# A hand-planned attention and two-layer kernel: weight preparation moved from GpSimd to VectorE, batch 0 turned with a diagonal factor, and a planner with other costs

## The chip, the core and the metric

The kernel runs on one core of one Trainium2 chip. A core has TensorE (PE), VectorE (DVE), ScalarE (ACT), GpSimd (POOL) and SyncE (SP), which issues the transfers here. Each engine takes its instructions in the order in which they were written. The metric is device time in microseconds (us) for one launch, lower is better: the median of the runs shown. A difference of about 0.5% is what a measurement of this kernel can tell from none.

## What is computed

```python
# q, k, v: (4, 12, 448, 64) fp32; w_in: (768, 2048); w_out: (2048, 768); alpha: (2048,)
scores = q @ k.T / 8
scores = cap * tanh(scores / cap)
attn   = exp(scores - max(scores)); attn = attn / (sum(attn) + 1e-9)
x      = (attn @ v) with the heads side by side        # (1792, 768)
h      = x @ w_in
g      = max(h, 0) + alpha * min(h, 0)
out    = g @ w_out                                     # (1792, 768)
```

The weights come as 64-bit floats, which the kernel reads as pairs of 32-bit integers.

## The kernel before

**Stages.** The four batches go through attention, then the first product (`mm1`), then the second (`mm2`). Attention works on pairs of heads, six pairs ("units") a batch. Batches 1 to 3 (`attention`) use fp16 pairs, a high and a low part of each number: q and k are scaled and split into `nat`, turned by a transfer into `qkTs`, multiplied on TensorE (L713), put through tanh (L501), row maximum (L506), exp (L513) and a factor per row (L518, L520). The weighted rows are split into `pw` (three buffers), turned by transfers into `ptall`, and multiplied with v (L585). Batch 0 (`attention32`) stays in fp32: q and k are turned on TensorE (L447, L448), the scores are fp32 products (L654), the rows of exp are scaled in place by their factor (in `steps`, `scaled`, L376 on VectorE), turned on TensorE against the identity (`turn_32`, L550), copied out of PSUM (L368) and multiplied with v (L599).

**Weights.** Each of the 16 chunks of `w_in` and of `w_out` is loaded as integers into `wp` and made into fp32 by `to_f32`: a shift and a mask (L826), the sign (L830), and the lowest bits. The lowest bits come in one of two ways: "fused", one VectorE instruction (L836), or a shift on VectorE (L839) and an add on GpSimd (L841). Then `split_w` makes an fp16 pair of each chunk, again in one of two ways: "direct" (the high part from the scaled chunk, L374 or L376, and the low part in one VectorE instruction with two inputs, L382), or scaled in place, copied (L368 or L370) and subtracted on GpSimd (L379). The constants XI, XO, AI and AO say which share of the chunks goes the fused or direct way: 0 and 0.25 for the bits of w_in and w_out, 0 and 0.75 for their splits. The scale of all w_out chunks (`s_wo`, L933) needs every chunk's norm, so `mm2` can't start before all of them are converted.

**What sets the order.** Every operation goes into a list by `Plan.op` with a priority, the engines that may do it, an assumed duration on each, and the regions that it reads and writes. `Plan.order` then plays the engines forward in time with these durations: a free engine takes the ready operation of the smallest number, an operation that ACT or POOL could do too is put back on DVE by PEN or PEN2, and the order found is the order in which the instructions are emitted. A wrong duration does no harm to the result, but the order is then made for another time table than the chip's. While the planned time is below FILL_END (87 us) and TensorE has nothing to do, the planner puts in "fills" (L980): small fp16 products of the identity with itself that nobody reads.

Of the kernel before, what the change touches and what calls it, by code (L numbers as in the profile page):

```python
# [29 lines left out]
PEN = 114.44  # L30
PEN2 = 133.12
B0_P = -3.48
LD_P = 2.02
LO_P = -51.36
MM_P = 203.41
X_P = 1.06
ST_P = 0.96
ST1_P = 5.53
PV_P = 22.36
QK_P = 10.39  # L40
V_P = 16.33
WI_P = 18.58
WI_S = 5.11
A_S = 7.06
MM1_P = 0.37
WO_P = 102.99
WO_S = 1.76
WT_P = 137.29
WT_S = 3.72
B1_P = 75.7  # L50
B_S = 31.76
EVAC_P = 57.51
# [5 lines left out]
XI = 0  # L58
XO = 0.25
AI = 0  # L60
AO = 0.75
# [3 lines left out]
FILL_END = 87045.86  # L65
# [10 lines left out]
class Plan:  # L76
# [15 lines left out]
    def op(self, prio, times, fn, r=(), w=(), rows=1.0):  # L92
        o = lambda: None
        o.prio, o.times, o.fn, o.rows, o.idx = prio, times, fn, rows, len(self.ops)
# [24 lines left out]
    def order(self):  # L119
# [6 lines left out]
        warm, win, busy = False, 0, 0.0  # L126

# [34 lines left out]
        while todo:  # L162
# [10 lines left out]
            for e in free:  # L173
# [3 lines left out]
                while ready[e]:  # L177
# [54 lines left out]
def kernel(  # L232
# [79 lines left out]
    mxt = ct([NF, 128], F32, "mxt")  # L312
    vs16 = ct([P, 2, 2, 2 * NCH * D], F16, "vs16")
# [28 lines left out]
    def allmax(prio, src, rows, r, first, w):  # L342
# [14 lines left out]
        op(prio, {"dve": 350}, reduce, r=[h], w=[tr])  # L357
        op(prio, {"pe": 100}, lambda e: nc.tensor.matmul(  # L358
            ps_p[h.slot][:, 256:256 + m], ones[:m], diag if m > 1 else top, start=True, stop=True), r=[tr], w=[h])
        op(prio, {"dve": 100}, lambda e: first(ps_p[h.slot][:, 256:256 + m]), r=[h], w=w)  # L360
# [60 lines left out]
    def vbatch(b):  # L421
# [8 lines left out]
        for pair in range(NPAIR):  # L430
# [3 lines left out]
            op(prio + 0.4 * pair, {"dve": 600}, lambda e, pair=pair, rv=rv: absmax(t[:CP, pair:pair + 1], rv),  # L434
               r=[m], w=[(u.tok, pair, pair + 1)])
# [41 lines left out]
    def steps(u, prio, n, S_, s_ns, sr_, scale, dma):  # L477
# [3 lines left out]
        for i0 in range(0, nb, 2):  # L481
# [15 lines left out]
            else:  # L497
# [3 lines left out]
            op(pr, {"act": 90 + 400 * m}, lambda e, s=s, t=t, m=m: nc.scalar.activation(  # L501
# [14 lines left out]
            op(pr, {"act": 735 * m}, exp, r=[mr], w=tr + [(("sums", u.idx % 3), c, c + 1) for c in blocks])  # L516
# [11 lines left out]
    blk_no = [0]  # L528
# [15 lines left out]
    def turn_32(u, pr, c, t, tr):  # L544
# [483 lines left out]
```

## Time and profile before

| what | value |
|---|---|
| median of 3 runs | 784.52 us (783.15 to 786.89) |
| the profiled execution | 784.08 us, its span from the first instruction to the last 782.3 us |
| busy in the span | PE 704.1, DVE 563.7, ACT 451.8, POOL 207.3 us |
| mean granted clock of TensorE | 0.954 of full speed |

The span is cut below at three marks: 261 us, when the scale of w_out is ready; 291 us, when the last chunk of w_out is split; 360 us, when the first product of batch 1 with w_in starts. Busy times are shares of the span and say nothing on which engine was waited for; the rows on the chain that ended last and on single waits do. A matmul's end is modelled in the trace, so for TensorE only stretches are summed.

### The profile page before, as it was taken

What the parts mean: (1) busy time and instruction counts of PE and PEld (TensorE: products, weight loads), DVE (VectorE), ACT (ScalarE), POOL (GpSimd) and SP (SyncE); (2) the same over time, 40 slices, a digit from 0 to 9 for tenths busy, and PEclk for the clock granted to TensorE, in tenths of its full rate; (3) what the DMA queues carried; (4) which work ended last, traced back from release to release, by engine and by line L of the source; (5) the groups of instructions that cost most, each with busy time, mean ns of one, the idle gap of its engine ahead of it and who ended that gap; (6) DMA issues with size and microseconds to landing.
All of it is one profiled execution on the core that took longest, in us unless ns stands there. A gap on an engine that the chain in (4) does not pass through costs nothing. (4 is left out here: it accounts for less than half of the span.)

```text
span 782.3 us, 12555 instructions
## 1 busy us (share of the span) xinstructions
PE 704.1 (90%) x4532; PEld 415.2 (53%) x4532; DVE 563.7 (72%) x1200; ACT 451.8 (58%) x877; POOL 207.3 (27%) x217
## 2 busy tenths in 40 slices
PE   8988967898988588959999999899999999999997
PEld 5646544476765245534444455455445555555664
DVE  4799997999998997887899877459879741443000
ACT  3767665798754874757686666457765821332010
POOL 1478463656653221100333300002222100000000
PEclk9999977899999689988999999999999999999999
DMA  9984523368775439997588887798658760000001
GB/s 212 241 256 126 169 75 100 107 149 175 176 172 126 91 75 175 205 177 160 113 135 158 157 171 148 144 173 143 107 110 146 130 116 20 21 1 1 21 21 40
DMA packets 227933, 98.61 MB, mean 126 GB/s; under 512 B 191456, under 2 KB 224160, under 8 KB 227872
## 3 DMA queue, kind: packets, MB, share of 16 engines
q1 hardware_dynamic: 227872, 97.82, 59.0%
q8 instruction: 35, 0.57, 0.3%
q14 instruction: 26, 0.21, 0.1%
HBM read 45.82 MB, written 5.51 MB: 66 GB/s over the span
## 5 line engine op out<-in xcount | busy, mean ns | idle before, releaser
L730 PE MATMUL p<-xring,wi 128*128 128x448 f16 (+2 forms) x1440 | 229.8, 319 | 3.6 <-POOL wi L379 2.5
L771 PE MATMUL p<-wp,gall 128*128 128x384 f16 x1344 | 227.9, 330 | 4.4 <-POOL wp L379 2.0
L730 PEld LDWEIGHTS <-wi 128*128 128x128 f16 x1440 | 138.0, 99 | 87.7 <-issue 4.7
L771 PEld LDWEIGHTS <-gall 128*128 128x128 f16 x1344 | 131.2, 99 | 95.7 <-issue 11.7
L513 ACT ACTIVATE tall<-tall,mxs,small 128x448 f32<-128x448 f32 x126 | 94.3, 750 | 22.2 <-POOL mxs L508 21.7
L382 DVE SCALAR_TENSOR_TENSOR pw<-tall,rr,pw 128x448 f16<-128x448 f32 x126 | 91.2, 737 | 12.5 <-ACT pw L374 12.1
L508 POOL TENSOR_SCALAR mxs<-mxs,small 128x2 f32<-128x2 f32 (+1 forms) x85 | 37.8, 444 | 229.0 <-DVE mxs L506 183.2
L379 POOL TENSOR_TENSOR gall<-gr,gall 128x192 f16<-128x192 f32 (+4 forms) x62 | 58.5, 947 | 115.5 <-ACT gall L368 73.8
L740 DVE SCALAR_TENSOR_TENSOR gr<-p,ca_g,gr 128x448 f32<-128x448 f32 (+2 forms) x80 | 46.5, 582 | 53.5 <-ACT gr L374 53.5
L374 ACT ACTIVATE pw<-tall,rr 128x448 f16<-128x448 f32 x95 | 61.8, 661 | 38.4 <-DMA ptall<-pw 25.4
L506 DVE TENSOR_REDUCE mxs<-tall 128x2 f32<-128x896 f32 x72 | 68.1, 957 | 17.5 <-ACT tall L501 17.5
L713 PE MATMUL s<-qkTs 128*128 128x448 f16 (+1 forms) x288 | 63.2, 384 | 19.3 <-DMA qkTs<-nat 18.5
L501 ACT ACTIVATE tall<-s,ams 128x896 f32<-128x896 f32 (+1 forms) x72 | 64.2, 904 | 24.5 <-PE s L713 22.8
L374 ACT ACTIVATE gr<-p,cs_g 128x448 f32<-128x448 f32 (+2 forms) x66 | 35.4, 537 | 46.8 <-PE p L730 44.9
L368 ACT ACTIVATE gall<-gr 128x384 f16<-128x384 f32 (+4 forms) x76 | 32.9, 438 | 40.4 <-DVE gr L740 40.4
L585 PE MATMUL p<-ptall,vs 112*64 112x448 f16 (+1 forms) x456 | 47.9, 352 | 2.2 <-DMA ptall<-pw 0.9
L374 ACT ACTIVATE wp<-p,small 128x384 f32<-128x384 f32 x20 | 11.5, 577 | 65.4 <-PE p L771 65.4
L713 PEld LDWEIGHTS <-qkTs 128*128 128x128 f16 (+1 forms) x288 | 22.8, 105 | 49.0 <-DMA qkTs<-nat 22.3
L654 PE MATMUL s<-tall,qkTs 128*128 128x448 f32 x84 | 39.6, 596 | 0.3 <-DVE qkTs L370 0.3
L841 POOL TENSOR_TENSOR wi<-wi,wp 128x768 int32<-128x768 int32 x14 | 33.2, 2377 | 20.1 <-DVE wp L839 15.5
L585 PEld LDWEIGHTS <-vs 112*64 112x64 f16 x456 | 26.0, 111 | 22.7 <-issue 7.6
L841 POOL TENSOR_TENSOR wp<-wp,wp 128x768 int32<-128x768 int32 x14 | 27.7, 1981 | 22.5 <-DVE wp L839 8.6
(145 smaller groups left out, 920.5 us busy)
## 6 DMA issues: line engine op xcount, KB each, us to landing
wp<-in_moe_w_in_dram SPq DMA_DIRECT2D x16, 768.0 KB, 5.9
wp<-in_moe_w_out_dram SPq DMA_DIRECT2D x16, 768.0 KB, 4.5
rvs<-in_v_dram SPq DMA_DIRECT2D x38, 224.0 KB, 3.2
rqk<-in_q_dram SPq DMA_DIRECT2D x18, 224.0 KB, 3.1
rqk<-in_k_dram SPq DMA_DIRECT2D x18, 224.0 KB, 3.5
ptall<-pw SPq DMA_TRANSPOSE x148, 3.3
wp<-in_k_dram SPq DMA_DIRECT2D x6, 224.0 KB, 7.8
wp<-in_q_dram SPq DMA_DIRECT2D x6, 224.0 KB, 8.3
```

The source lines that it names most:

```text
L374: nc.scalar.activation(out=o, in_=i, func=AF.Copy, scale=s)
L379: (nc.gpsimd if e == "pool" else nc.vector).tensor_tensor(out=o, in0=a, in1=b, op=ALU.subtract)
L382: nc.vector.scalar_tensor_tensor(out=o, in0=i, scalar=s, in1=hi, op0=ALU.mult, op1=ALU.subtract)
L501: op(pr, {"act": 90 + 400 * m}, lambda e, s=s, t=t, m=m: nc.scalar.activation(out=t, in_=s[:, :m, :S].rearrange("p c (j k) -> p c j k", j= ...
L506: op(pr, {"dve": 20 + 490 * m}, lambda e, mt=mt, t=t: nc.vector.tensor_reduce(out=mt, in_=t, axis=AX.XY, op=ALU.max), r=tr, w=[mr])
L513: nc.scalar.activation(out=t[:, x], in_=t[:, x], func=AF.Exp, scale=capt, bias=mt[:, x:x + 1], accum_out=u.sums[:, c:c + 1])
L585: nc.tensor.matmul(pv[x * D:(x + 1) * D, :n], vs[:, z, c:c + D], u.pt[x][:CP, y * NCH + kc], start=(i == 0), stop=(i == len(prods) - 1))
L713: nc.tensor.matmul(s[rows], qT[:, x * S + cols.start:x * S + cols.stop], qkT[:, r0:r0 + NCH, :], start=(z == 0), stop=(z == 1))
L730: nc.tensor.matmul(ps_p[h.slot][:, :n], w[:, z, kk, :], x[:, d, o:o + n], start=(kk == 0 and z == d), stop=(kk == NPAIR - 1 and z == 1))
L740: op(pr, {"dve": 80 + 1.15 * n}, lambda e: nc.vector.scalar_tensor_tensor(out=t, in0=ps_p[h.slot][:, :n], scalar=ca_g[:, j:j + 1], in1=t, ...
L771: nc.tensor.matmul(ps_p[h.slot][:, :NH], g[j][:, d, t * P:(t + 1) * P], w[:, z, hf * NH:(hf + 1) * NH], start=(j == 0 and z == d), stop=(j ...
L841: op(prio, {"pool": 1760}, lambda e: nc.gpsimd.tensor_tensor(out=f, in0=f, in1=lo, op=ALU.add), r=[sr], w=[fr])
```

## The change

`to_f32` and `split_w` go the fused and the direct way for every chunk (XI, XO, AI and AO are 1), so GpSimd has no weight work left. In batch 0 the row factor is no longer multiplied into the rows: `turn_32` makes a diagonal matrix of the factors (`diags`, four buffers, by ACT or DVE), and the turn is a matmul of the rows with this diagonal in place of a transpose against the identity. `Plan.order` keeps for DVE and POOL the time until which an operation of theirs occupies a shared port: a POOL operation starts after the DVE operation that holds it, and DVE skips operations marked as using it while POOL runs. Operations that read PSUM and reductions are marked `port=False`. Almost all assumed durations are changed, the priorities are another set of numbers, and FILL_END is 467.8 us in place of 87 us.

```diff
-PEN = 114.44
+PEN = 472.85
...
-XI = 0
-XO = 0.25
-AI = 0
-AO = 0.75
+XI = 1
+XO = 1
+AI = 1
+AO = 1
...
-FILL_END = 87045.86
+FILL_END = 467838.18
...
+        port = {"dve": 0.0, "pool": 0.0}
...
-                    if not fits(o):
+                    if not fits(o) or e == "dve" and o.port and port["pool"] > now:
...
+                        if e == "pool":
+                            free[e] = end = port[e] = max(now, port["dve"]) + t
+                        elif e == "dve" and o.port:
+                            port[e] = end
...
-            op(pr, {"dve": 130, "pool": 290}, lambda e, mt=mt: (nc.gpsimd if e == "pool" else nc.vector).tensor_scalar(
+            op(pr, {"dve": 200, "pool": 440}, lambda e, mt=mt: (nc.gpsimd if e == "pool" else nc.vector).tensor_scalar(
...
-                    op(pr, {"dve": 370}, lambda e, x=x, t=t, r=r: scaled(e, t[:, x], t[:, x], r[:, x:x + 1]), r=[rt], w=tr)
-                    turn_32(u, pr, c, t[:, x], tr)
+                    turn_32(u, pr, n, c, t[:, x], tr, r[:, x:x + 1], rt)
...
+        d, dr = diags[:, i], ("dg", i, i + 1)
+        op(pr, either(P), lambda e: scaled(e, d, ident, f), r=[identr, fr], w=[dr])
...
-                nc.tensor.transpose(ps_p[h.slot][:CP, j * P:(j + 1) * P], t[:, j], ident)
+                nc.tensor.matmul(ps_p[h.slot][:CP, j * P:(j + 1) * P], t[:, j], d, start=True, stop=True)
...
-        op(pr, {"pe": 450}, turn_P, r=tr + [identr], w=[h, ptw])
+        op(pr, {"pe": 4 * (P / 0.6 + 30)}, turn_P, r=[*tr, dr], w=[h, *ptw])
...
-        op(prio, {"pool": 1600, "dve": 880}, lambda e: minus(e, dst[:, DM:], flat, dst[:, :DM]), r=[fr, high], w=[low])
+        op(prio, {"pool": 1990, "dve": 945}, lambda e: minus(e, dst[:, DM:], flat, dst[:, :DM]), r=[fr, high], w=[low])
```

Line numbers move by 7 to 11: L839 and L841 are gone or moved (the sign is L841 now, the fused bits L847), the direct low part is L389, the row maximum's scaling L515, the diagonal L381 or L383, the turn L560, the fill L991.

**VectorE, around the conversion of the w_in chunks `wi_85` to `wi_87`.** Before:

```order
L839 TENSOR_SCALAR wp_95<-wp_95 128x768
L891 RECIPROCAL s_wi<-iv_wi 128x2
L826 TENSOR_SCALAR wi_86<-wp_96 128x768
L826 TENSOR_SCALAR wi_87<-wp_93 128x768
L830 SCALAR_TENSOR_TENSOR wi_86<-wp_96,wi_86 128x768
L518 TENSOR_SCALAR rr<-sums 128x2
L338 TENSOR_REDUCE n_wi<-p_66 128x2
L520 RECIPROCAL rr<-rr 128x2
L839 TENSOR_SCALAR wp_96<-wp_96 128x768
L376 TENSOR_SCALAR gall<-gall,rr 128x4x112
```

After:

```order
L837 TENSOR_SCALAR wi_86<-wp_96 128x768
L902 RECIPROCAL s_wi<-iv_wi 128x2
L345 TENSOR_REDUCE small<-rqk 112x1
L841 SCALAR_TENSOR_TENSOR wi_86<-wp_96,wi_86 128x768
L513 TENSOR_REDUCE mxs<-ptall 128x1
L847 SCALAR_TENSOR_TENSOR wi_86<-wp_96,wi_86 128x768
L345 TENSOR_REDUCE small<-rqk 112x1
L389 SCALAR_TENSOR_TENSOR wi_81<-wi_83,s_wi,wi_81 128x768
```

The shift L839 is replaced by the fused L847, the scaling of batch 0's rows (`gall<-gall,rr`) is gone, and the low parts of the split (L389) have come to VectorE.

**GpSimd, the same stretch.** Before:

```order
L508 TENSOR_SCALAR mxs<-mxs,small 128x1
L841 TENSOR_TENSOR wi_85<-wi_85,wp_95 128x768
L639 MEMSET qkTs 64x64
L841 TENSOR_TENSOR wi_86<-wi_86,wp_96 128x768
L379 TENSOR_TENSOR wi_79<-wi_81,wi_79 128x768
L379 TENSOR_TENSOR wi_80<-wi_82,wi_80 128x768
L841 TENSOR_TENSOR wi_87<-wi_87,wp_93 128x768
L508 TENSOR_SCALAR mxs<-mxs,small 128x2
```

After:

```order
L650 MEMSET qkTs 64x64
L515 TENSOR_SCALAR mxs<-mxs,small 128x1
L515 TENSOR_SCALAR mxs<-mxs,small 128x2 x16
L386 TENSOR_TENSOR gall<-gr,gall 128x192 x6
L515 TENSOR_SCALAR mxs<-mxs,small 128x1
```

Between the last small memset and the first low part of `g` (`gall`) GpSimd now has only the scaling of row maxima (`mxs`). Over the whole program the 48 weight instructions are gone, and `mxs` counts 93 in place of 85, the low parts of `g` 80 in place of 62.

**TensorE, between the last product of batch 0 with w_in (`wi_92`) and the first with w_out.** Before:

```order
L730 MATMUL p_63<-xring,wi_92 128x256
L850 LDWEIGHTS wp_100
L850 MATMUL p_64<-wp_100 128x128
...
L355 MATMUL p_65<-ident,n_wi 16x128
L358 MATMUL p_65<-mxt,ones 128x16
L355 MATMUL p_66<-ident,small 2x112
L358 MATMUL p_66<-mxt,ones 128x2
L771 LDWEIGHTS gall
```

After:

```order
L741 MATMUL p_64<-xring,wi_92 128x256
L991 LDWEIGHTS ident
L991 MATMUL p_65<-ident 128x128
...
L724 MATMUL s_62<-qkTs 128x448
...
L861 MATMUL p_66<-wp_100 128x128
...
L362 MATMUL p_63<-ident,n_wi 16x128
```

Fills (L991) and scores of batch 1 (L724) now stand there. Over the whole program there are 790 fills in place of 142; all of them stand ahead of the second product of batch 1 with w_in.

## Rows read from the trace of the kernel before

**Rows 1.** Busy time by stage: the stretch, its length, busy us and instructions of PE, PEld, DVE, ACT and POOL, the granted TensorE clock, the DMA share and GB/s.

```profile
0.00:261.00 261.00, 218.39 (x1650) 153.57 (x1650) 235.78 (x458) 177.60 (x362) 136.82 (x123) 0.92 0.61 156
261.00:291.00 30.00, 21.41 (x97) 10.57 (x99) 28.62 (x54) 22.91 (x32) 10.44 (x7) 0.72 0.56 106
291.00:360.00 69.00, 58.08 (x369) 30.72 (x365) 52.56 (x126) 43.24 (x84) 6.70 (x12) 0.93 0.94 178
360.00:783.00 423.00, 406.20 (x2419) 220.38 (x2419) 246.73 (x566) 208.04 (x402) 53.39 (x75) 1.00 0.53 100
```

**Rows 2.** The chain of work that ended last, its first and its last pieces: start us, us, what.

```profile
564.64 0.75 ACT tall L513 x2
...
664.51 51.07 PE p L730 x270
715.59 62.41 PE p L771 x384
```

**Rows 3.** The marks in the timeline: start us, us, instruction. The scale of w_out, the last split of w_out, and the first product of batch 1.

```profile
261.34 0.23 DVE L933 SCALAR_TENSOR_TENSOR s_wo<-iv_wi,small,sg 128x16 f32<-128x16 f32 x1
289.68 1.00 DVE L382 SCALAR_TENSOR_TENSOR wp<-wp,s_wo,wp 128x768 f16<-128x768 f32 x1
360.25 2.07 PE L730 MATMUL p<-xring,wi 128*128 128x448 f16 x10
```

**Rows 4.** Timeline of DVE and POOL from 94 to 107 us: start us, us, instruction, and the idle time before it.

```profile
94.14 0.95 DVE L830 SCALAR_TENSOR_TENSOR wi<-wp,wi 128x768 int32<-128x768 int32 x1
95.37 0.22 DVE L353 TENSOR_SCALAR mxt<-ident,mxt 2x2 f32<-2x2 f32 x1
95.51 0.43 DVE L376 TENSOR_SCALAR gall<-gall,rr 128x448 f32<-128x448 f32 x1
96.52 1.65 POOL L379 TENSOR_TENSOR wi<-wi,wi 128x768 f16<-128x768 f32 x1 [3.96 <-issue]
96.93 1.66 DVE L839 TENSOR_SCALAR wp<-wp 128x768 int32<-128x768 int32 x1
104.22 0.15 DVE L518 TENSOR_SCALAR rr<-sums 128x2 f32<-128x2 f32 x1
105.30 0.54 DVE L826 TENSOR_SCALAR wp<-wp 128x768 int32<-128x768 int32 x1
106.19 0.54 DVE L839 TENSOR_SCALAR wp<-wp 128x768 int32<-128x768 int32 x1
```

**Rows 5.** Groups on DVE in the first 261 us, shapes apart: line, operation, out<-in, count | busy us, mean ns | idle before.

```profile
L376 DVE TENSOR_SCALAR gall<-gall,rr 128x448 f32<-128x448 f32 x31 | 21.5, 700 | 0.0
L830 DVE SCALAR_TENSOR_TENSOR wp<-wp,wp 128x768 int32<-128x768 int32 x18 | 20.3, 1129 | 0.0
L839 DVE TENSOR_SCALAR wp<-wp 128x768 int32<-128x768 int32 x28 | 18.7, 666 | 0.0
L382 DVE SCALAR_TENSOR_TENSOR pw<-tall,rr,pw 128x448 f16<-128x448 f32 x17 | 16.1, 950 | 0.0
L830 DVE SCALAR_TENSOR_TENSOR wi<-wp,wi 128x768 int32<-128x768 int32 x14 | 16.0, 1145 | 0.0
L506 DVE TENSOR_REDUCE mxs<-gall 128x2 f32<-128x896 f32 x15 | 15.9, 1068 | 0.2 <-ACT gall L501 0.2
L826 DVE TENSOR_SCALAR wp<-wp 128x768 int32<-128x768 int32 x18 | 14.3, 796 | 0.0
L518 DVE TENSOR_SCALAR rr<-sums 128x2 f32<-128x2 f32 x26 | 10.9, 422 | 2.0 <-ACT gall L513 1.6 <-ACT ptall L513 0.2
L826 DVE TENSOR_SCALAR wi<-wp 128x768 int32<-128x768 int32 x14 | 10.8, 778 | 0.9 <-DMA wp<-in_moe_w_in_dram 0.9
L353 DVE TENSOR_SCALAR mxt<-ident,mxt 2x2 f32<-2x2 f32 x11 | 6.9, 631 | 0.5
L376 DVE TENSOR_SCALAR ptall<-ptall,rr 128x448 f32<-128x448 f32 x7 | 5.1, 726 | 0.0
L686 DVE SCALAR_TENSOR_TENSOR ams<-ams,small 128x1 f32<-128x1 f32 x3 | 3.5, 1181 | 0.0
```

**Rows 6.** Groups on DVE from 300 to 640 us, in the same columns.

```profile
L382 DVE SCALAR_TENSOR_TENSOR pw<-tall,rr,pw 128x448 f16<-128x448 f32 x102 | 69.1, 692 | 12.5 <-ACT pw L374 12.1 <-ACT tall L501 0.2
L518 DVE TENSOR_SCALAR rr<-sums 128x2 f32<-128x2 f32 x42 | 8.1, 194 | 2.7 <-ACT tall L513 2.3
L686 DVE SCALAR_TENSOR_TENSOR ams<-ams,small 128x1 f32<-128x1 f32 x13 | 3.5, 269 | 0.0
```

**Rows 7.** Groups on POOL in the first 360 us, in the same columns: work that stays there.

```profile
L508 POOL TENSOR_SCALAR mxs<-mxs,small 128x2 f32<-128x2 f32 x37 | 17.2, 464 | 97.9 <-DVE mxs L506 81.7 <-DVE rr L520 6.0 <-DVE iv_wi L859 4.2
L379 POOL TENSOR_TENSOR gall<-gr,gall 128x192 f16<-128x192 f32 x15 | 12.5, 834 | 10.5 <-ACT gall L368 9.9 <-DVE pw L382 0.5
L379 POOL TENSOR_TENSOR gall<-gr,gall 128x256 f16<-128x256 f32 x12 | 11.2, 932 | 15.5 <-ACT gall L368 15.5
```

**Rows 8.** Timeline of PE, four runs: two runs of fills, the turn of one block of batch 0 (four transposes of 128 columns), and a step of fp32 scores (four records are two matmuls of 448 columns).

```profile
1.69 2.85 PE L980 MATMUL p<-ident 128*128 128x128 f16 x25 [1.69 <-POOL ident masks.py:199]
16.32 1.40 PE L980 MATMUL p<-ident 128*128 128x128 f16 x22
34.57 0.65 PE L550 MATMUL p<-ident,gall 128*112 128x128 f32 x4
111.00 1.67 PE L654 MATMUL s<-tall,qkTs 128*128 128x448 f32 x4
```

More of the change, by code (lines that the diff above doesn't have):

```diff
@@ L29 @@
 AQ = 3
-PEN = 114.44
[L31 to L52, printed above, removed]
+PEN = 472.85
+PEN2 = 254.09
+B0_P = -15.83
+LD_P = -3.98
+LO_P = -119.89
+MM_P = 334.69
+X_P = 15.73
+ST_P = -5.85
+ST1_P = 13.86
+PV_P = 65.33
+QK_P = 18.37
+V_P = 42.05
+WI_P = 31.04
+WI_S = 6.37
+A_S = 14.49
+MM1_P = 6.72
+WO_P = 118.15
+WO_S = 9.38
+WT_P = -3.52
+WT_S = -13.71
+B1_P = 124.3
+B_S = 32.74
+EVAC_P = 205.47
 LAT = 200.0
@@ L90, in handle, with op @@
         return h
-    def op(self, prio, times, fn, r=(), w=(), rows=1.0):
+    def op(self, prio, times, fn, r=(), w=(), rows=1.0, port=True):
         o = lambda: None
-        o.prio, o.times, o.fn, o.rows, o.idx = prio, times, fn, rows, len(self.ops)
+        o.prio, o.times, o.fn, o.rows, o.idx, o.port = prio, times, fn, rows, len(self.ops), port
         o.handles, deps = [], set()
@@ L356, in allmax @@
            r=[*r, identr], w=[h])
-        op(prio, {"dve": 350}, reduce, r=[h], w=[tr])
+        op(prio, {"dve": 480 if m > 1 else 260}, reduce, r=[h], w=[tr], port=False)
         op(prio, {"pe": 100}, lambda e: nc.tensor.matmul(
             ps_p[h.slot][:, 256:256 + m], ones[:m], diag if m > 1 else top, start=True, stop=True), r=[tr], w=[h])
-        op(prio, {"dve": 100}, lambda e: first(ps_p[h.slot][:, 256:256 + m]), r=[h], w=w)
+        op(prio, {"dve": 150}, lambda e: first(ps_p[h.slot][:, 256:256 + m]), r=[h], w=w, port=False)
     def share(i, x):
@@ L572, in split_v @@
         return vs, vt
-    two = {"act": 620, "dve": 400}
+    two = {"act": 710, "dve": 485}
     def PV_split(u, prio, n, vs, vt):
@@ L629, in attention32 @@
             rk, rkr = raw32[4, pair]
-            op(prio, {"pe": 520}, lambda e, h=h: turn(h, rk, 0, NCH), r=[rkr, identr], w=[h], rows=0.7)
-            op(prio, either(S, True), lambda e, h=h: copy(e, kt[:, pair, :], ps_p[h.slot][:, :S]), r=[h], w=[ktr])
+            op(prio, {"pe": 960}, lambda e, h=h: turn(h, rk, 0, NCH), r=[rkr, identr], w=[h], rows=0.7)
+            op(prio, either(S, True), lambda e, h=h: copy(e, kt[:, pair, :], ps_p[h.slot][:, :S]), r=[h], w=[ktr], port=False)
         h = plan.handle("a")
@@ L639, in attention32 @@
             op(prio, {"pool": 140}, lambda e: nc.gpsimd.memset(qzs[qi][D:, PART[0][1]:PART[1][1]], 0.0), w=[qzr[qi]])
-        op(prio, {"pe": 130 * nch}, lambda e, h=h: turn(h, rq, c0, nch), r=[rqr, identr], w=[h, qr], rows=0.7)
+        op(prio, {"pe": 240 * nch}, lambda e, h=h: turn(h, rq, c0, nch), r=[rqr, identr], w=[h, qr], rows=0.7)
         z = qz.rearrange("p (h t) -> p h t", h=2)
@@ L694, in attention @@
         both = nat[:CP, 2 * NCH:]
[L695 removed]
+        op(pr, {"dve": 420}, lambda e: nc.vector.tensor_copy(both[:, :, D:], both[:, :, 0:D]), w=[nt[1], nt[2]])
         qkT = qkTs[:, u.idx % 2]
@@ L784, in mm2 @@
         op(EVAC_P + prio * 1e-4, either(NH, True), lambda e: scaled(e, osb[:, cols], ps_p[h.slot][:, :NH], osc),
-           r=[h, *oscs], w=[osr])
+           r=[h, *oscs], w=[osr], port=False)
         last = b == B - 1 and t == 3
```

77 lines of the change are left out of this document (40 added, 37 removed).

## The prediction

> **What bounds the kernel now.** I began with the chain that ended last: it begins at 564.6 us, and from then on is nearly all TensorE [rows 2]. The end is a TensorE end, so the question is when TensorE gets its work. The busy times by stage answer that [rows 1]. From the mark at 360 us, the first product of batch 1 [rows 3], TensorE is busy 406.2 of the 422 us left, at a granted clock of 1.00: that part costs what its products cost. Ahead of 360 us it is different: TensorE is idle 62 of 360 us (360 - 218.4 - 21.4 - 58.1), and its clock is 0.92, 0.72 and 0.93 of full speed, that is, for part of each stretch it runs at 1.2 in place of 2.4 GHz. There VectorE is the full engine: 235.8 of 261 us and 28.6 of the next 30, against 177.6 and 22.9 on ACT. All the conversions of both weights, batch 0 and the six units of batch 1 pass through it, and the scale of w_out at 261.3 us is itself a VectorE instruction [rows 3].
>
> Part of that VectorE time is no work. In the timeline a mask of 768 columns takes 0.54 us (L839 at 106.19), and 1.66 us when a GpSimd instruction began just ahead of it (L839 at 96.93, POOL from 96.52 to 98.17) [rows 4]. The groups of the first 261 us show how much: the waits are in the groups' means [rows 5]. Reductions show none: L506 takes 1,068 ns.
>
> **The change part by part.** I sum VectorE's time up to the mark at 360 us, since all work that the change touches lies ahead of it.
>
> 1. *Port waits that go.* Mean in [rows 5] less the duration of the same form when free [rows 4, 6], times count: L376 on `gall` 31 x (0.70 - 0.43) = 8.4; L830 on `wp` and `wi` 18 x 0.18 + 14 x 0.20 = 6.0; L839 28 x 0.13 = 3.5; L382 on `pw` 17 x 0.26 = 4.4; L826 18 x 0.26 + 14 x 0.24 = 8.0; L518 26 x 0.27 = 7.1; L353 11 x 0.41 = 4.5; L376 on `ptall` 7 x 0.30 = 2.1; L686 3 x 0.91 = 2.7. That is 47 us; the groups not shown are smaller and of the same sign, and I take **50 us** (47 is the low end, and for the high end I allow 57).
>
> 2. *Port waits that stay.* Ahead of the mark GpSimd keeps 53 scalings of row maxima and 32 low parts of g, by [rows 7] 53 x 0.46 + 16 x 0.83 + 16 x 0.93 = 53 us, 16% of some 330 us. L518 serves as a gauge: with GpSimd busy 52% of the time (136.8 of 261) its excess is 0.27 us, and 0.04 us (0.194 - 0.15) in the later stretch [rows 6], where GpSimd is busy 13% (53.4 of 423) [rows 1]. Between these, 16% gives about a fifth of the 50 us: **10 us** stay (ends: 5 if only the low parts of g count, 26 below).
>
> 3. *VectorE work that goes and comes.* Batch 0's scaling goes: 38 x 0.43 = -16.3; one of 38 diagonals comes to VectorE, +0.2. Twenty-eight chunks exchange the shift (0.54) for a fused instruction with two inputs, priced as L830 (0.95): 28 x 0.41 = +11.5. Sixteen low parts of w_in and four of w_out come at the 1.00 us of L382 [rows 3]: +20; two copies of high parts go, -1.1 by L839's 0.54. Sum **+14 us**. What moves between ACT and VectorE otherwise I put at nothing: ACT loses 14 copies and gains 37 diagonals by the order, and it has 84 us to spare in the first 261 [rows 1].
>
> 4. *The rest of the wait ahead of the mark.* From 291 to 360 us VectorE has 16 us of idle time. The order carries attention of batch 1 further ahead of the w_out scale than before, so less of it is left in this stretch; I take a quarter, **-4 us**.
>
> So the mark moves from 360.3 to 360.3 - 50 + 10 + 14 - 4 = **330 us**, if VectorE sets it throughout.
>
> 5. *TensorE ahead of the mark.* Two terms. A turn of one block, four times 128 columns, takes 0.65 us as transposes [rows 8]; as an fp32 product the nearest row is the score product, 1.67 us for 896 columns, so 512 columns give 0.95 us: 38 x 0.30 = +11 us. (The Trainium skill, TensorE: Matmul & The Clock Gate, in Terms, says that the transpose mode is four times faster for FP32; by that, from the same row, the turn would take 2.6 us and the 38 would add 74 us. The score row stands for the product itself, so I keep 0.95.) The fills are 648 more: 0.064 us each by the run of 22, 0.114 by the run of 25 in the first microseconds [rows 8], so 41 to 74 us; I take 41, since fills are issued where the clock is to stay up. TensorE's 298 us ahead of the mark hold time at the low clock: (0.08 x 261 + 0.28 x 30 + 0.07 x 69) = 34 us of the stretches. Without it 264, with both terms 316 us. That is under 330, so both lie beside VectorE's work; but only 14 us under, and if that cover is gone each further microsecond of fills costs one.
>
> 6. *Behind the mark.* 422 us, of which 406 are busy. The products are the same, no fills stand there, and VectorE and ACT have slack (247 and 208 of 423 us), so their table of durations matters little. TensorE's 17 us of idle time include the end of the last copy and transfer; I give back **4 us**.
>
> The sum: 330 + 422 - 4 = 748 us of span. The profiled execution has 1.8 us around its span (784.08 - 782.3), so 750; it is 0.4 us below the median of 784.52, which changes nothing. **I forecast 750 us**, 4.4% less. A change within 0.5% (3.9 us) is what a measurement of this kernel can't tell from none.
>
> **The rivals.**
>
> *The port waits come back with other partners (767 us).* Every one of the 85 GpSimd instructions that stay ahead of the mark catches a VectorE instruction once, in its middle: their mean is 53 / 85 = 0.62 us, so 85 x 0.31 = 26.5 us stay, not 10: 750 + 17 = 767. For it: the low parts that came to VectorE have two inputs in SBUF, and L382 on `pw`, which has two, is among the forms that waited [rows 5]. Against: with GpSimd at 13% the same form loses nearly nothing, 692 ns [rows 6]. Beside it stands the Trainium skill, SBUF — State Buffer, Who interferes with whom: the shared ports are an exclusive lock, whichever starts first holds them for its whole instruction, and a VectorE instruction with two SBUF inputs is subject to it. By that rule this rival is the plain case; the trace agrees on reductions, which never waited.
>
> *The order fits the chip better than I count (726 us).* Fills and true durations bring back what stages 261 to 360 lose, too: of VectorE's 43 us of idle time ahead of the mark (25 + 1 + 16, [rows 1]) 17 more go, and behind the mark 7 of TensorE's 17: 750 - 24 = 726. For it: the clock of 0.72 and the waits around the w_out splits [rows 1] go with no engine full but VectorE. Against: the loads and the turning transfers (a DMA share of 0.94 from 291 to 360) are the same.
>
> *The fills and diagonals land on TensorE's path (803 us).* The engine takes its fills in order; if they are planned for a pause that on the chip comes elsewhere, it does the fills and then still waits. Price: 41 + 11 = 52 us, all of it on the path: 750 + 53 = 803. It decides from 38 us on: above that the kernel is slower than 788.4. For it: 14 us of margin is little (point 5), a fill that needs a bank waits for the engine that empties it, and everything behind it waits too. Against: the planner puts a fill only where no product is ready, with durations that are now near the rows here (2.0 us for L841, 0.54 for a mask).
>
> *No change (784 us).* The batch 1 units, not VectorE, set the mark: turning transfers with three buffers, the DMA share of 0.94, hold it where it is. Against: those units start earlier too, and VectorE was 91% busy until 291 us.
>
> **How the numbers follow.** The forecast has 0.45, the port rival 0.17, the better fit 0.22, the fills on the path 0.10, no change 0.06. The predicted time is the forecast's. Its own bounds: point 1 from 47 to 57, point 2 from 5 to 10, points 4 and 6 each nothing to twice: 738 to 761. The range takes in the port rival and its surroundings and most of the better fit: **722 to 778**; outside are the slower case, no change, and an end of the better fit. Faster by over 0.5%: 0.45 + 0.17 + 0.22 = 0.84. Within 0.5%: 0.06. Slower: 0.10.
>
> **What would show it.** The mark of the first batch 1 product at about 330 us; `rr` (L525) near 0.19 us and the masks near 0.54 us in the first 250 us; VectorE still over 90% busy there; a granted clock near 1.00 up to the mark; the stretch behind the mark 415 to 420 us. Wrong, if TensorE is over 95% busy ahead of the mark with fills in front of late products (the fills' rival), or if the L847 and L389 groups stand well over 0.95 and 1.00 us (the port rival).

## The result, and the profile after

The kernel after takes **762.93 us** (median of 4 runs, 762.52 to 763.3) against 783.84 us (4 runs) for the kernel before on the same chip: a ratio of 0.9729, 95% interval 0.9697 to 0.9761. The forecast was 750, the range 722 to 778. The profiled execution took 763.0 us, its span is 761.1 us, against 782.3 before.

The same cut of the span as in [rows 1], made at after's own marks (stretch, length, busy us and records of PE, PEld, DVE, ACT, POOL, granted clock, DMA share, GB/s):

```profile
0.00:271.00 271.00, 252.36 (x2210) 191.90 (x2211) 216.80 (x483) 189.95 (x403) 52.99 (x89) 0.96 0.71 169
271.00:295.00 24.00, 24.00 (x223) 16.42 (x222) 23.80 (x46) 21.76 (x34) 2.46 (x3) 1.00 0.37 79
295.00:355.00 60.00, 59.41 (x495) 36.95 (x493) 43.10 (x102) 40.23 (x78) 8.41 (x12) 1.00 0.92 176
355.00:762.00 407.00, 401.02 (x2412) 219.49 (x2409) 227.44 (x518) 200.49 (x392) 61.94 (x93) 1.00 0.54 100
```

The three marks of [rows 3], from the timelines of DVE and PE (start us, us, instruction):

```profile
271.05 0.23 DVE L944 SCALAR_TENSOR_TENSOR s_wo<-iv_wi,small,sg 128x16 f32<-128x16 f32 x1
292.93 1.94 DVE L389 SCALAR_TENSOR_TENSOR wp<-wp,s_wo,wp 128x768 f16<-128x768 f32 x2
355.24 0.92 PE L741 MATMUL p<-xring,wi 128*128 128x448 f16 x4
```

The second row holds the last two splits of w_out; the last one starts at 293.9 us. The first product of batch 1 starts at 355.2 us: 5 us earlier than before, not 30. The scale of w_out comes 10 us *later* than before. Behind the mark there are 406 us, where there were 422: 16 us less, not 4. The VectorE row has changed sides: it was full up to 291 us, and now it is busy 217 of the first 271 us, 80%, while TensorE is at 93, 100 and 99%.

The groups on VectorE in the first 271 us answer to [rows 5] (line, operation, out<-in, count | busy us, mean ns | idle before):

```profile
L841 DVE SCALAR_TENSOR_TENSOR wp<-wp,wp 128x768 int32<-128x768 int32 x18 | 17.0, 945 | 0.0
L847 DVE SCALAR_TENSOR_TENSOR wp<-wp,wp 128x768 int32<-128x768 int32 x18 | 17.0, 945 | 0.0
L389 DVE SCALAR_TENSOR_TENSOR pw<-tall,rr,pw 128x448 f16<-128x448 f32 x24 | 16.6, 694 | 3.8 <-ACT pw L381 3.8
L389 DVE SCALAR_TENSOR_TENSOR wi<-wi,s_wi,wi 128x768 f16<-128x768 f32 x14 | 13.8, 1010 | 0.5 <-ACT wi L381 0.5
L837 DVE TENSOR_SCALAR wp<-wp 128x768 int32<-128x768 int32 x18 | 9.7, 545 | 3.3 <-DMA wp<-in_moe_w_out_dram 3.3
L837 DVE TENSOR_SCALAR wi<-wp 128x768 int32<-128x768 int32 x14 | 7.7, 547 | 0.0
L525 DVE TENSOR_SCALAR rr<-sums 128x2 f32<-128x2 f32 x29 | 5.3, 182 | 0.3 <-ACT gall L520 0.2
L360 DVE TENSOR_SCALAR mxt<-ident,mxt 2x2 f32<-2x2 f32 x14 | 3.0, 217 | 0.5
```

VectorE's waits for GpSimd are gone from these groups: the sign takes 945 ns where it took 1,129, the mask 545 where it took 796, `rr` 182 where it took 422, `mxt` 217 where it took 631. On TensorE, the fills and the turns of batch 0 over the whole span (the same columns, PE's tiles with the weights' shape), and four blocks' turns in the timeline, which answer to [rows 8]:

```profile
L991 PE MATMUL p<-ident 128*128 128x128 f16 x790 | 52.8, 224 | 2.2 <-POOL ident masks.py:199 1.7 <-DVE n_wi L345 0.5
L560 PE MATMUL p<-diags,gall 128*112 128x128 f32 x248 | 31.2, 278 | 2.1 <-ACT ptall L375 2.0
L560 PE MATMUL p<-diags,ptall 128*112 128x128 f32 x56 | 6.8, 273 | 0.0
```

```profile
105.24 3.70 PE L560 MATMUL p<-diags,gall 128*112 128x128 f32 x32
```

The fills are 52.8 us of TensorE. A product with the diagonal takes 3.70 us for four blocks (two records are one product of 128 columns), 0.92 us a block.

Over the whole span TensorE explains the difference: it was busy 704.1 us and idle 78.2, and is now busy 736.8 and idle 24.3. Idle time has lost 53.9 us. Busy time has grown by 32.7: fills +40.1 (52.8 against 12.7), turns of batch 0 +12.1 (38.0 against 25.9), all else -19.5, at a granted clock of 0.983 against 0.954. -53.9 + 32.7 = -21.2 us, the difference of the spans.

### The profile page after: what moved, and what is told of

It reads as the page before. It is cut to its first block, busy times and chain, and to the rows that moved or that the text cites. A ratio compares the mean times of both kernels' runs of the same rounds, so it can differ in the third digit from the quotient of the medians.

```text
span 761.1 us, 14048 instructions
## 1 busy us (share of the span) xinstructions
PE 736.8 (97%) x5332; PEld 464.8 (61%) x5332; DVE 511.1 (67%) x1146; ACT 452.4 (59%) x903; POOL 125.8 (17%) x197
## 4 chain that ended last, share of the span: by engine, by line
PE 83%; DVE 5%; DMA 4%; ACT 4%; issue 2%; POOL 0%; SPq 0%; ACTq 0%; POOLq 0%
PE p L782 28%; PE p L741 24%; PE s L724 5%; PE p L596 5%; PE p L991 5%; PE s L665 4%; PE p L560 4%; DMA ptall<-pw 3%; PE p L610 2%; PE p L455 2%; DVE mxs L513 1%; PE p L861 1%; PE p L365 1%; PE p L454 1%; DVE pw L389 1%
## 5 line engine op out<-in xcount | busy, mean ns | idle before, releaser
L782 PE MATMUL p<-wp,gall 128*128 128x384 f16 x1344 | 225.2, 326 | 0.0
L515 POOL TENSOR_SCALAR mxs<-mxs,small 128x2 f32<-128x2 f32 (+1 forms) x93 | 45.9, 493 | 319.0 <-DVE mxs L513 202.1
L389 DVE SCALAR_TENSOR_TENSOR pw<-tall,rr,pw 128x448 f16<-128x448 f32 x126 | 85.5, 688 | 17.6 <-ACT pw L381 17.4
L386 POOL TENSOR_TENSOR gall<-gr,gall 128x384 f16<-128x384 f32 (+4 forms) x80 | 66.6, 842 | 167.2 <-ACT gall L375 101.6
L381 ACT ACTIVATE pw<-tall,rr 128x448 f16<-128x448 f32 x98 | 63.1, 660 | 43.7 <-DMA ptall<-pw 39.6
L513 DVE TENSOR_REDUCE mxs<-tall 128x2 f32<-128x896 f32 (+1 forms) x72 | 69.0, 961 | 5.3 <-ACT tall L508 4.8
L724 PE MATMUL s<-qkTs 128*128 128x448 f16 (+1 forms) x288 | 61.4, 360 | 6.3 <-ACT tall L508 6.2
L381 ACT ACTIVATE gr<-p,cs_g 128x448 f32<-128x448 f32 (+2 forms) x60 | 32.9, 549 | 53.2 <-PE p L741 48.8
L381 ACT ACTIVATE wp<-p,small 128x384 f32<-128x384 f32 x23 | 13.3, 580 | 75.0 <-PE p L782 74.9
L991 PE MATMUL p<-ident 128*128 128x128 f16 x790 | 52.8, 224 | 2.2 <-POOL ident masks.py:199 1.7
L991 PEld LDWEIGHTS <-ident 128*128 128x128 f16 x790 | 48.3, 100 | 6.5 <-issue 2.4
L375 ACT ACTIVATE gall<-gr 128x384 f16<-128x384 f32 (+4 forms) x85 | 35.8, 434 | 25.3 <-DVE gr L751 25.0
L724 PEld LDWEIGHTS <-qkTs 128*128 128x128 f16 (+1 forms) x288 | 22.3, 101 | 28.8 <-issue 15.6
L596 PEld LDWEIGHTS <-vs 112*64 112x64 f16 x456 | 25.9, 110 | 21.2 <-issue 7.5
## 6 DMA issues: line engine op xcount, KB each, us to landing
wp<-in_q_dram SPq DMA_DIRECT2D x6, 224.0 KB, 10.3
```

The costliest lines, as they stand in the source:

```text
L381: nc.scalar.activation(out=o, in_=i, func=AF.Copy, scale=s)
L386: (nc.gpsimd if e == "pool" else nc.vector).tensor_tensor(out=o, in0=a, in1=b, op=ALU.subtract)
L389: nc.vector.scalar_tensor_tensor(out=o, in0=i, scalar=s, in1=hi, op0=ALU.mult, op1=ALU.subtract)
L513: op(pr, {"dve": 136 + 469 * m}, lambda e, mt=mt, t=t: nc.vector.tensor_reduce(out=mt, in_=t, axis=AX.XY, op=ALU.max), r=tr, w=[mr], port= ...
L596: nc.tensor.matmul(pv[x * D:(x + 1) * D, :n], vs[:, z, c:c + D], u.pt[x][:CP, y * NCH + kc], start=(i == 0), stop=(i == len(prods) - 1))
L724: nc.tensor.matmul(s[rows], qT[:, x * S + cols.start:x * S + cols.stop], qkT[:, r0:r0 + NCH, :], start=(z == 0), stop=(z == 1))
```

## The experiments

The tables of a plan and the work that it orders were changed together, so most runs change one and keep the other. "Mark" is the start of batch 1's first product with w_in; "behind" is the rest of the span. Ratios are to the kernel before on the same chip. The runs stand on several chips, on which the kernel before takes 781.5 to 784.9 us, so the ratios compare runs better than the times; mark and behind come from one profiled execution each.

| run | us | ratio, 95% interval | mark | behind |
|---|---|---|---|---|
| before (profiled) | 784.08 | 1 | 360.3 | 422.0 |
| after | 762.93 | 0.9729 (0.9697 to 0.9761) | 355.2 | 405.9 |
| after, 142 fills | 752.62 | 0.9613 (0.9563 to 0.9663) | 347.1 | 406.6 |
| after, 288 fills of one pause left out | 758.47 | 0.9680 (0.9632 to 0.9729) | 351.9 | 404.1 |
| before + weights | 786.96 | 1.0026 (0.9993 to 1.0058) | 360.1 | 426.0 |
| before + diagonal turn | 785.66 | 1.0016 (0.9988 to 1.0043) | 363.0 | 421.9 |
| before + both | 769.28 | 0.9857 (0.9802 to 0.9912) | 343.0 | 424.5 |
| work of before, plan of after, 142 fills | 803.45 | 1.0282 (1.0239 to 1.0325) | 393.2 | 409.3 |
| after, priorities of before, 142 fills | 769.83 | 0.9847 (0.9798 to 0.9896) | 356.7 | 412.6 |
| after, no port in the planner, 142 fills | 769.53 | 0.9844 (0.9799 to 0.9890) | 353.6 | 414.2 |
| after, other latency, 142 fills | 754.48 | 0.9650 (0.9596 to 0.9705) | 346.9 | 409.5 |
| after, other split cost, 142 fills | 758.19 | 0.9679 (0.9618 to 0.9741) | 350.7 | 405.2 |
| after, weights back, 142 fills | 788.19 | 1.0070 (1.0039 to 1.0102) | 380.1 | 406.2 |
| after, transposes back, 142 fills | 761.46 | 0.9733 (0.9681 to 0.9784) | 356.2 | 403.5 |

### What the fills cost

The order of after, with only its first 142 fills issued:

```diff
     def fill(slot):
+        fill_no[0] += 1
+        if fill_no[0] > 142:
+            return
```

> The changed kernel in the same order, but only its first 142 fills are issued (as many as before the change). After the change the chain that ended last runs through 5% of its span in fills (38 us), and w_out's scale comes at 271 us. Theory 'fills on the path': the 648 fills left out give back most of their 43 us (0.067 us each): 725 to 750 us. Rival 'fills only fill pauses': 760 to 766 us. Rival 'fills pay by the clock': the granted clock falls to about 0.95 or lower and the time rises to 768 to 785 us.

It took 752.62 us, faster than both kernels: fills on the path is the nearest of the three cases, though the time lies above its 725 to 750. In the profile TensorE is busy 713.1 us and idle 40.6 of a span of 753.7 us. Its groups of fills, to be held against L991 above:

```profile
L996 PE MATMUL p<-ident 128*128 128x128 f16 x142 | 11.9, 254 | 1.7 <-POOL ident masks.py:199 1.7
```

So the 648 fills take 40.9 us of TensorE (52.8 - 11.9). They save 17.2 us of other busy time (40.9 less the difference of the busy times, 23.7), at a clock of 0.983 in place of 0.969, and they lie in 16.3 us of time that is idle without them. 40.9 - 17.2 - 16.3 = 7.4 us are left on the path, and that is the difference of the spans; the mark moves by 8.1 us. The profiled execution is the slowest of the four of this run (755.45 us against 752.43 to 752.78), so 7.4 us is a low value: the medians differ by 10.3 us, the ratios by 9. That the 17.2 us come from the clock is a reading of the two clock figures.

The longest runs of fills stand between batch 0's last product with w_in and the first with w_out. The chain that ended last in after goes through them (start us, us, what; this is a part of it):

```profile
254.66 1.97 PE p L741 x18
256.63 4.75 PE p L991 x85
261.38 0.38 PE s L724 x2
261.75 4.08 PE p L991 x73
265.83 0.34 PE p L861 x6
```

Read as causes, those rows say that the norm at 265.8 us waits for 73 fills. The next run leaves the 288 fills of this pause out:

```diff
+        fill_no[0] += 1
+        if 309 < fill_no[0] <= 597:
+            return
```

> The changed kernel in the same order, without the 288 fills between the last product of batch 0 with w_in and the first with w_out; the other 502 stay. 'Fills on the path': the last norm of w_out no longer stands behind 158 fills, its scale comes 8 to 15 us ahead of 271 us, the time is 746 to 756 us. 'Only pauses': 761 to 765 us, the scale at 269 to 272 us. 'Clock': the clock between 256 and 300 us falls below 0.9 and the time is 764 us or more.

It took 758.47 us, between the first two cases, and the scale of w_out comes where the second had it, at 270.79 us against 271.05 in after:

```profile
269.17 0.68 DVE L389 SCALAR_TENSOR_TENSOR pw<-tall,rr,pw 128x448 f16<-128x448 f32 x1
270.79 0.23 DVE L944 SCALAR_TENSOR_TENSOR s_wo<-iv_wi,small,sg 128x16 f32<-128x16 f32 x1
```

The fills of the pause did not hold up the scale: a chain that is followed to the instruction before it on the same engine names what stood there, not what was waited for. The scale waits for the conversion and the norm of the last chunk of w_out, whose instructions take turns on VectorE with batch 1's `pw` (the first row above).

Behind the scale the fills did hold something up. The last products with v ahead of w_out, what follows them, and the first products with w_out, in after and then without the 288 fills:

```profile
272.92 2.46 PE L596 MATMUL p<-ptall,vs 112*64 112x448 f16 x24
275.31 3.41 PE L991 MATMUL p<-ident 128*128 128x128 f16 x58
278.56 4.06 PE L782 MATMUL p<-wp,gall 128*128 128x384 f16 x24
```

```profile
270.86 4.21 PE L596 MATMUL p<-ptall,vs 112*64 112x448 f16 x24
275.00 1.48 PE L782 MATMUL p<-wp,gall 128*128 128x384 f16 x8
```

The stretch around that in the columns of [rows 1], again in after and then without:

```profile
240.00:300.00 60.00, 59.85 (x629) 45.82 (x628) 53.60 (x106) 42.43 (x72) 9.50 (x16) 1.00 0.63 118
```

```profile
240.00:300.00 60.00, 51.73 (x363) 32.59 (x361) 53.89 (x108) 44.89 (x77) 10.08 (x16) 0.89 0.58 118
```

The granted clock is 1.00 with the fills and 0.89 without, and the 24 products with v take 2.46 us in place of 4.21, but they start 2.1 us later. Then 58 fills stand in front of the first product with w_out, which starts at 278.6 us with the fills and at 275.0 without; the mark is 3.4 us later (355.2 against 351.9). So in this pause the fills lose in front of products what they bring by the clock, and over 3 us more. By the spans these 288 fills account for 5.1 us (756.0 against 761.1) and the other 360 for 2.3; by the medians it is 4.5 and 5.9, so only the sum is firm.

### One part of the work at a time, with the old plan

The kernel before, with the weights alone (first run) and with the diagonal turn alone (second):

```diff
-XI = 0
-XO = 0.25
-AI = 0
-AO = 0.75
+XI = 1
+XO = 1
+AI = 1
+AO = 1
```

```diff
-                    op(pr, {"dve": 370}, lambda e, x=x, t=t, r=r: scaled(e, t[:, x], t[:, x], r[:, x:x + 1]), r=[rt], w=tr)
-                    turn_32(u, pr, c, t[:, x], tr)
+                    turn_32(u, pr, n, c, t[:, x], tr, r[:, x:x + 1], rt)
...
-                nc.tensor.transpose(ps_p[h.slot][:CP, j * P:(j + 1) * P], t[:, j], ident)
+                nc.tensor.matmul(ps_p[h.slot][:CP, j * P:(j + 1) * P], t[:, j], d, start=True, stop=True)
```

> The kernel before with XI, XO, AI and AO at 1 alone (old priorities, old durations, transposes, fills up to 87 us). If the port waits on VectorE are the bound ahead of the mark (50 us go, 31 us of VectorE work come): 764 to 770 us, with rr (L518) near 0.19 us. Rival 'the order decides': taken off GpSimd under the old durations the work comes at the wrong places, 780 to 800 us, although the waits are gone.

> The kernel before with the diagonal turn of batch 0 alone. If VectorE bounds: 16 us of its work go, 768 to 776 us. Rival 'TensorE's 11 us more and the longer chain exp, factor, diagonal, product count': 784 to 796 us.

Neither moves the time (1.0026 and 1.0016), and both come out where the rivals had them. Both bring the scale of w_out earlier, by 13 and 17 us against [rows 3], and the mark stays at 360 and 363 us. The two rows of each, weights first:

```profile
248.52 0.23 DVE L933 SCALAR_TENSOR_TENSOR s_wo<-iv_wi,small,sg 128x16 f32<-128x16 f32 x1
360.08 0.54 PE L730 MATMUL p<-xring,wi 128*128 128x448 f16 x2
```

```profile
244.78 0.23 DVE L938 SCALAR_TENSOR_TENSOR s_wo<-iv_wi,small,sg 128x16 f32<-128x16 f32 x1
362.97 0.55 PE L735 MATMUL p<-xring,wi 128*128 128x448 f16 x2
```

VectorE is idle 68 and 54 us ahead of these marks, where it was 43 before: it has room to spare. From these two I formed the theory that the plan brings the whole gain. The next four runs were made to test it.

### Work and plan, four corners

Both parts of the work together in the kernel before, with the old plan (the two diffs above; the order found has 68 fills); and the opposite corner, the kernel after with the work of before (both diffs reversed, the turn planned at 650 ns and the scaling at 430) and 142 fills:

> The kernel before with both changes of the work (all chunks fused and direct, batch 0 turned with its diagonal) and nothing of the new plan: old priorities, old durations, no port in the planner, fills until 87 us. Theory 'work': each part alone left the mark at 360 to 363 us only because the other part still filled VectorE; together the mark falls to 340 to 345 us and the time to 765. Theory 'plan': batch 1's units stand where the old order puts them; the scale of w_out comes by 240 us or earlier, but the mark stays at 357 to 363 us and the time at 781 to 788.

> The other corner: the kernel after with the work of before (XI, XO, AI, AO back, batch 0 scaled in place and turned by transposes), planned anew with the new priorities, the new durations and the port in the planner, and with the first 142 fills only, so it stands against the run with 142 fills (752.6 us). Theory 'plan': the order alone brings the gain: 750 to 762 us, the mark below 352 us, 404 to 412 us behind it. Theory 'work': the port waits come back (GpSimd busy 200 us or more, masks well over 0.54 us in the mean), VectorE is full again up to 300 us, and the time is 775 or more.

The theory fell, from both sides. Together the two parts bring 1.4% with the old plan, where each alone brought nothing; and the new plan with the old work is 2.8% *slower* than before. With the run of 142 fills as the fourth corner the table reads: old work 1 and 1.028 (old and new plan), new work 0.986 and 0.961. The plan takes 2.4% of the time of before off the new work and adds 2.8% to the old. One rival is open in the 1.4%: that run has 74 fills fewer than before, which are 6.3 us of TensorE (6.4 against 12.7), and how much of this was on the path was not run.

Where the plan's part lies is seen in TensorE's waits (who waited <- for what: us in total, times, longest). The plan is compared at 142 fills, since the 790 of after would hide waits. First before + both up to 360 us, then after with 142 fills:

```profile
PE s L718 <- DMA qkTs<-nat: 26.7, 5, 13.5
PE p L359 <- DVE mxt L354: 6.1, 5, 3.0
PE p L356 <- DVE n_wi L339: 2.8, 1, 2.8
```

```profile
PE s L724 <- ACT tall L508: 10.4, 4, 4.2
PE p L861 <- DVE wp L847: 5.8, 3, 3.0
PE s L724 <- DMA qkTs<-nat: 0.9, 1, 0.9
```

With VectorE relieved and the old order, the scores wait 26.7 us for the transfers that turn their q and k (`qkTs<-nat`). The longest of these waits, 13.5 us, is that of batch 2's first unit: seven units' scores (112 of 288 records, 16 a unit) stand ahead of the mark, and the seventh ahead of batch 1's last product with v:

```profile
334.26 4.36 PE L718 MATMUL s<-qkTs 128*128 128x448 f16 x14 [13.47 <-DMA qkTs<-nat]
338.55 2.46 PE L590 MATMUL p<-ptall,vs 112*64 112x448 f16 x24
```

In the kernel before the same wait was 12.9 us:

```profile
PE s L713 <- DMA qkTs<-nat: 12.9, 5, 7.2
PE p L358 <- DVE mxt L353: 11.8, 9, 2.6
```

The relief that VectorE got was in part turned into this wait; with the order of after it is 0.9 us. Ahead of the mark the plan does not gain by that: TensorE's idle time falls from 47.5 to 34.7 us, but its busy time grows from 295.5 to 312.4, 5.5 of it fills, and the mark comes 4.1 us later. The gain is behind the mark, where idle time falls from 17.8 to 5.9 us and busy time from 406.8 to 400.7. The largest wait there, first of before + both, then of after with 142 fills:

```profile
PE s L718 <- DMA qkTs<-nat: 7.7, 8, 1.7
```

```profile
PE s L724 <- ACT tall L508: 0.9, 1, 0.9
```

In time, the three steps from 782.3 us of span are: both parts of the work -14.8 (mark -17.3, behind the mark +2.5), the plan -13.8 with 142 fills (mark +4.1, behind it -17.9), the 648 other fills +7.4. By the ratios they are some 11 and 19 us less and 9 us more: the signs are the same, the sizes good to some 5 us.

### Which part of the plan

After with the 23 priorities of before; after without the planner's port; each planned anew, with 142 fills:

```diff
-PEN = 472.85
+PEN = 114.44
...
-EVAC_P = 205.47
+EVAC_P = 57.51
```

```diff
-                    if not fits(o) or e == "dve" and o.port and port["pool"] > now:
+                    if not fits(o):
...
-                        if e == "pool":
-                            free[e] = end = port[e] = max(now, port["dve"]) + t
-                        elif e == "dve" and o.port:
-                            port[e] = end
```

> The kernel after with the 23 priority numbers of before, but its own work, durations and port in the planner, and the first 142 fills only; it stands against 752.6 us. If the priorities carry the plan's gain: 775 to 785 us, the stretch behind the mark back at 420 us. If the measured durations carry it: 750 to 758 us. I hold the priorities the likelier, since with the same work old durations and old priorities together gave no gain.

> The kernel after without the planner's port (GpSimd and VectorE planned as if they never waited for each other), all else kept, and the first 142 fills only; it stands against 752.6 us. With GpSimd busy 17% the port is hardly contended, so I expect 750 to 757 us, no difference that counts. If the port in the plan matters, the masks and the rr group (183 ns after) grow again and the time is 760 or more.

Both come out at 770 us, 17 us above the 752.6 that they stand against. For the priorities that is about what I expected, between the two cases; for the port I had expected no difference. But an edit of the planner gives another order, and the 17 us could be no more than the price of leaving the order that the numbers were fitted to. Two controls change one number of no importance:

```diff
-LAT = 200.0
+LAT = 202.0
```

```diff
-    two = {"act": 710, "dve": 485}
+    two = {"act": 717, "dve": 490}
```

> A control for the runs at 770 us: the kernel after with 142 fills (752.6 us) whose planner assumes 202 ns in place of 200 ns from one engine to the next, and is otherwise the same; the order found differs in many places. Theory 'this plan only': the 23 priorities were fitted to one order, any other order found with them loses what the port and the old priorities seemed to lose: 762 to 775 us. Theory 'the port and the priorities count': a plan with both keeps 748 to 758 us.

> A second control of the same kind: the durations of the scaled copy of q, k and v in the planner are 717 and 490 ns in place of 710 and 485, all else as in the kernel after with 142 fills. 'This plan only': 762 to 775 us. 'The port and the priorities count': 748 to 758 us.

754.48 and 758.19 us, the second at the very edge of what I had set for it: by these two controls another order costs 2 to 6 us, so both the priorities and the port count beyond that. What the port in the planner does is for the most part not the avoiding of waits on the chip: without it the masks of w_out take 613 ns in the mean, the signs 962 and the lowest bits 990, so these 3 x 18 instructions lose 2.3 us against after, and with the low parts of w_out (1,052 ns for 1,006) and of q and k (778 for 745) it is some 4 us of VectorE. The mark is 6.5 us later and the rest 7.6 us longer. Which of the changed places in the order carries this I did not isolate.

### Which part of the work, with the new plan

After with the weights back on GpSimd (the diff of XI to AO reversed), and after with batch 0's scaling and transposes back (the diff of the turn reversed), both with 142 fills:

> The kernel after, 142 fills, with the weights alone back on GpSimd as before (XI 0, XO 0.25, AI 0, AO 0.75), planned anew with the port in the planner; the diagonal turn stays. Both parts back gave 803 us against 752.6. If the planner's port makes VectorE stand by for every GpSimd instruction, so that GpSimd's long weight instructions are what this planner can't place, then the weights carry most of the 51 us: 785 to 800 us. If the two parts count alike, 775 to 780 us; if the plan can cope, below 765 us.

> The kernel after, 142 fills, with batch 0 scaled in place on VectorE and turned by transposes as before, planned anew (turn 650 ns, scaling 430 ns); the weights stay off GpSimd. If the weights carry most of the 51 us: 755 to 765 us. If the two parts count alike, 775 to 780 us. TensorE saves 38 x 0.27 us = 10 us of turns here, so a time below 752 us would show that the diagonal costs more than it brings in this plan.

The weights carry most: 788.19 us, 36 above the 752.6. The transposes back give 761.46, 9 us above, of which the spread of the controls (up to 6) is a part. In the run with the weights back the whole loss lies ahead of the mark (380.1 us against 347.1; behind it 406.2 and 406.6). Its first 300 us, and the same of before, in the columns of [rows 1]; first before:

```profile
0.00:300.00 300.00, 248.80 (x1810) 169.38 (x1811) 273.33 (x530) 207.49 (x408) 149.06 (x132) 0.90 0.60 149
```

```profile
0.00:300.00 300.00, 245.23 (x1853) 176.12 (x1853) 220.81 (x500) 191.29 (x390) 128.30 (x134) 0.89 0.64 153
```

Groups on VectorE in that stretch with the weights back, and its scale of w_out:

```profile
L850 DVE TENSOR_SCALAR wp<-wp 128x768 int32<-128x768 int32 x28 | 16.5, 588 | 0.0
L841 DVE SCALAR_TENSOR_TENSOR wi<-wp,wi 128x768 int32<-128x768 int32 x14 | 13.0, 943 | 0.0
L837 DVE TENSOR_SCALAR wi<-wp 128x768 int32<-128x768 int32 x14 | 7.5, 548 | 0.0
L389 DVE SCALAR_TENSOR_TENSOR pw<-tall,rr,pw 128x448 f16<-128x448 f32 x24 | 20.4, 867 | 1.1 <-ACT pw L381 1.1
```

```profile
303.01 0.23 DVE L944 SCALAR_TENSOR_TENSOR s_wo<-iv_wi,small,sg 128x16 f32<-128x16 f32 x1
```

GpSimd is busy 43% of this stretch, and VectorE's weight instructions hardly wait (548 to 588 ns where [rows 5] have 666 to 796 for these forms); `pw` still does, at 867 ns for the 694 of after. In place of most of the waits VectorE is idle, 79 us against 27 before, and the scale of w_out comes at 303 us in place of 261. My reading is that a planner that lets VectorE stand by for GpSimd turns the port's waits into idle time as long as GpSimd has long instructions; a run of this work without the port in the planner, which would show it, was not made.

## Why the prediction was right or wrong

The direction and the range held; the forecast of 750 us was 13 us too low. That the range held is in part luck: 762.9 us lies above the forecast's own bounds (738 to 761; added up as they are stated, the low end is 730) and inside the range by the room left for the port rival, which did not happen. The two halves of the sum were off in opposite directions: the mark 25 us later than forecast (355 against 330), the stretch behind it 12 us shorter (406 against 418).

*Points 1 to 3, VectorE's own sum: right.* I forecast -50 + 10 + 14 = -26 us of VectorE's busy time ahead of the mark. It went from 317.2 us before the mark of before to 283.9 before that of after, -33. The 10 us of waits that I let stay were too many: the means shown for after stand near the durations of the free forms in [rows 4, 6].

*Rival "port waits come back": no.* The low parts that came to VectorE take 1,010 ns (L389, against 1,000 in [rows 3]) and the sign 945 (against 950 in [rows 4]): neither waits. The Trainium skill, SBUF — State Buffer, Who interferes with whom, has the shared ports as an exclusive lock that the first to start holds. The runs here show that such a lock need not cost much where the two engines seldom meet: GpSimd is busy 53 of 271 us in after. They show no more, since the instructions' order decides who meets whom.

*"So the mark moves ... to 330 us, if VectorE sets it throughout": this step failed,* and with it the cover of point 5 ("both lie beside VectorE's work"). VectorE is busy 284 of the 355 us ahead of the mark, 80%. The engine that became the bound is TensorE: 336.0 busy of 355.2 us, 95%. I had it at 316 us. Both terms that I added were right, 41 and 11 us forecast, 40.1 and 12.1 measured, and the turn at 0.92 us a block for the 0.95 taken from the score row. What failed is the credit: I let all 34 us of the low clock come back, and TensorE's other work ahead of the mark shrank by 14 (298.1 + 40.1 + 12.1 - 336.0); the granted clock is still 0.96 in the first 271 us. The 34 us took the missing clock over the whole stretches, the 62 us included in which TensorE was idle. Over the whole span 19.5 us came back, and some 5 us of work that stood behind the mark came ahead of it. That is 20 of the 25 us. The other 5 are idle time of TensorE, 19 us where 14 were allowed.

*Rival "the fills and diagonals land on TensorE's path": in part.* Of its 52 us some 7 to 10 are on the path for the fills, and the sign that I had set for it was met to its edge: TensorE is 95% busy ahead of the mark, with 58 fills in front of the first product with w_out. I had put them all beside VectorE's work in the forecast and all on the path in the rival, and by the profiles the truth was a sum of three shares: clock 17, idle 16, path 7.

*Rival "no change": in part.* The conversions on VectorE did not set the mark any more once it had been relieved of one part of its work; two runs show the mark where it was, the scale of w_out 13 and 17 us earlier, and more of VectorE idle. That the units of batch 1 set it then is the reading that is left, not shown by a run of its own; the longest wait is that of batch 2's first unit, which the old order has ahead of them. With both parts the mark comes 17 us earlier.

*Point 4, -4 us: no.* From 295 to 355 us VectorE is idle 17 of 60 us, where it was 16 of 69 [rows 1].

*Rival "the order fits the chip better": half of it.* Behind the mark it asked for 11 us of TensorE's 17 idle ones (the forecast's 4 and its own 7), and 11 went. Ahead of the mark it asked for VectorE's idle time to shrink; that has grown, from 43 to 71 us.

*Point 6, behind the mark: mis-sized, 16 us for 4.* TensorE's idle time there fell from 16.1 to 5.1 us, and its busy time by 5.2 us (11 records fewer stand there). I had written that the table of durations matters little there, since VectorE and ACT have slack; the old plan with all of the new work still needs 424.5 us there, and the new one 406.6. The slack of the engines said nothing on the order: with the old plan the scores wait 7.7 us there for transfers, with the new one they don't.

*The diagonal.* The turn as a product costs 1.4 times the transposes (0.92 against 0.65 us in [rows 8]). The Trainium skill, TensorE: Matmul & The Clock Gate, Terms, calls the transpose mode four times faster for FP32; by the rows here it is not for this turn, and the measurement decides. In the new plan it seems worth its price: with the transposes back the time is 9 us longer, of which the spread between orders can make up to 6.

## What to carry to other kernels

When a full engine is relieved, sum the next engine up to the same mark with everything that the change adds to it, and give it back no clock or idle time that the rows don't show; each part of a relief can be worth nothing alone and something together. A plan and the work that it orders belong together: the same table of numbers was worth -2.4% with one set of work and +2.8% with the other, so neither is judged by itself, and a change of a planner is held against controls that change a number of no importance. Fills pay in three places at once (clock, idle time, path), and only leaving them out in the same order tells how much in each; those that stand in front of a product that is ready are lost time.

## What the runs showed of the hardware

The waits between VectorE and GpSimd shrink much faster than GpSimd's share. With GpSimd busy 136.8 of the first 261 us, `rr` took 422 ns; with 53.0 of 271 us it takes 182, nearly the 150 ns of the free instruction. With 128.3 of 300 us and an order that is planned to keep the two apart, masks and shifts take 548 to 588 ns, close to the free 540, while `pw` takes 867 for 694. GpSimd's side did not get shorter: its scalings of two row maxima, 464 ns in [rows 7], take 565 ahead of the mark of after; the trace does not say what they wait for.
